# Attention joined into two visits per chunk, with quarter-array state products, in a fused decay-attention and two-stage MoE kernel

## The chip, the core and the metric

The kernel runs on one core of one Trainium2 chip. The core has five engines: TensorE (PE in the profile, with PEld for its weight loads), VectorE (DVE), ScalarE (ACT), GpSimd (POOL) and SyncE (SP), whose queue issues most DMAs. The metric is the device time of one execution in microseconds (us), as the median of several runs.

## The reference

Attention with a decaying state feeds a dense squared-ReLU MLP, and that feeds a noisy top-2 mixture of eight experts:

```python
f = sigmoid(f_logit)                               # 4 batches, 8 heads, 768 steps, D = 48
for t in range(S):
    state = f[:, :, t, :, None] * state + einsum('bhd,bhe->bhde', k[:, :, t], v[:, :, t])
    y[:, :, t] = einsum('bhd,bhde->bhe', q[:, :, t], state)
x = y.transpose(0, 2, 1, 3).reshape(3072, 384)
h = maximum(x @ w_in, 0); x = (h * h) @ w_out      # 384 -> 2048 -> 384
noisy = x @ w_gate + log1p(exp(x @ w_noise)) * noise
# for each token its two largest experts, weighted by softmax: relu(x @ w1[e]) @ w2[e]
```

## The kernel before

**Tiling.** Tokens come in 24 chunks of 128 (`NCH`), six for each batch (`NCB`), and in eight blocks of three chunks (384 tokens, `NBLK`). Two heads share the 128 partitions as a pair, at partitions 0 to 47 and 64 to 111, and there are four pairs (`HP`).

**Attention of a chunk** is five pieces, `att_units(c)`: `a_A` (products of keys and queries, masked on VectorE into AM), `a_k` (transposes of the keys, copied by ScalarE into KT), `a_U` (the chunk's contribution to the state, then added and scaled on VectorE), `a_Y(c, 0)`, and `a_Y(c, 1)` followed by `a_S`. `a_Y` adds AM times values for half of the pairs each time; its second call also adds the products of the state `S_t` with the queries, which are full 128x128 matmuls, since `S_t` holds a pair's two states on its diagonal and zeros elsewhere. `a_S` refreshes `S_t`. The last chunk of a batch has no `a_k`, `a_U` and `a_S`, the first has no state product.

**The dense MLP** runs in units u: `mm1(u)` (nine matmuls into the bank mm, then r, g, gh on ScalarE and gl on VectorE) and `mm2(u - 2)` (nine matmuls into the banks a0 to a2). Each of the blocks 2 to 7 has 16 units. Up to u = 31 a list written out by hand, `ORDER`, sets the order of loads (W, E, V), weight conversion (A, H, B), preparation of chunks (P), attention pieces (a) and units (M). From u = 32 a loop does so: each unit calls `mm1`, then `attend`, which gives out one attention piece per unit, then `mm2`, then whatever `at` has put down for that unit. So a piece stands on TensorE between nine matmuls of `mm1` and nine of `mm2`: this is called a visit below. Chunk 10 is the first whose pieces all fall in the loop.

**Other steps** put down by `at`: `r_store` (VectorE turns a finished block into x2q, which is stored), `r_logits`, `r_logits2`, `r_exp`, `r_ln`, `r_choose`, `r_share`, `r_slots`, `r_scatter` (routing of the block's tokens, ending in six indirect DMAs from GpSimd), `check_load` and `check_step` (a test of the weights' words, one load and one VectorE step for each of 16 pieces), `zeros_out` and `pads` (fills in DRAM). `pads` writes small entries from a tile of the tag x2b, which `r_store`, `r_rows` and others share with one buffer.

**PSUM** has eight banks: mm twice, a0 to a2, and t0 to t2, which `abank` hands out in turn to attention and routing.

**Preparation** of a chunk: `prep_f`, then `prep_k` and `prep_F` (a scan on VectorE, and a small ScalarE copy FE of its result), `prep_G`, `prep_q` with `prep_Q` (on GpSimd).

Engines run their instructions in order, and so does SP's queue of DMAs.

Of the kernel before, what the change touches and what calls it, by code (L numbers as in the profile page):

```python
# [227 lines left out]
def kernel(  # L228
# [159 lines left out]
    def w_load(i):  # L388
# [8 lines left out]
        if kind == "in":  # L397
            for (r0, m, row0, rs) in ((0, 48, 0, 96), (64, 48, 48, 96), (48, 16, 288, 16), (112, 16, 336, 16)):
                s = bass.AP(tensor=w_in_v.tensor, offset=w_in_v.offset + row0 * DFF * WORDS + p * n,
                            ap=[[DFF * WORDS, m], [rs * DFF * WORDS, 3], [1, n]])  # L400
                nc.sync.dma_start(st[r0:r0 + m], s)
# [57 lines left out]
    phase = {"early": True}  # L459

    def abank(shape, dt=F32):
# [58 lines left out]
    def prep_F(c):  # L520
# [25 lines left out]
    def a_k(c):  # L546
        if c % NCB == NCB - 1:
            return
        pk = abank([128, HP, 128])
# [5 lines left out]
    def a_A(c):  # L555

        pA = [abank([128, HP, 128]) for s in range(2)]
# [10 lines left out]
    def a_U(c):  # L568
        if c % NCB == NCB - 1:
            return  # L570
        pU = abank([128, HP, D])
# [13 lines left out]
    def a_S(c):  # L585
        if c % NCB == NCB - 1:
            return
        for s in range(2):
            r = slice(64 * s, 64 * s + D)
            nc.scalar.activation(S_t[r, :, r], S_c[r], AF.Copy)  # L590

    pY = {}

    def a_Y(c, h):
        if h == 0:
            pY[c] = abank([128, HP, 128])
# [12 lines left out]
        if h == 1:  # L609
# [6 lines left out]
            if c >= 2 * BT:  # L616
                t = LP["p"].tile([128, HP, C], F32, tag="xs", name="xs", bufs=2)
                nc.scalar.activation(t, py, AF.Copy)
# [111 lines left out]
    def r_logits(j):  # L730

        pl = abank([128, BTOK])
# [5 lines left out]
    def r_logits2(j):  # L738
        pl = abank([128, BT, 96])
# [108 lines left out]
    def r_slots(j):  # L848
        oh, wt, ohb, cb, s12 = R[j]
        den = share_out(wt, s12, BT)  # L850
        pr = abank([128, BT, E])
# [345 lines left out]
    def pads():  # L1197
        t = mp.tile([128, NTL, E, 4], F32, tag="x2b", name="pads", bufs=1)
# [62 lines left out]

    if wide:
# [168 lines left out]
```

## Time and profile before

| what | value |
|---|---|
| median of 3 runs | 1038.68 us (1034.66 to 1039.46) |
| the profiled execution | 1035.95 us, span 1034.2 us |
| TensorE busy | 974.7 us (94% of the span), 6378 matmul instructions |
| VectorE, ScalarE, GpSimd busy | 617.0, 491.7, 183.0 us |
| mean granted TensorE clock | 0.976 of full speed |
| chain that ended last | PE 78%, DVE 6%, DMA 5%, SP's queue 4%, ACT 3% |

The span is the profiled part; 1.75 us lie around it. The chain follows the last instruction back through whatever released each step, so a share of 78% for PE says that most of the time the end was set by TensorE working through its own queue.

### The profile page before, as it was taken

To read this page: it belongs to the slowest core of one execution; us is meant where nothing else is said; L and a number is where in the kernel's file an instruction comes from. 1 tells how busy PE (TensorE), PEld (TensorE's weight loads), DVE (VectorE), ACT (ScalarE), POOL (GpSimd) and SP (SyncE) were. 2 spreads that over 40 slices of the span, in tenths; PEclk is the share of its full clock that TensorE was granted. 3 is DMA by queue.
4 is the path that set the end of the run, shared out by engine and by line. 5 is a ranking of instruction groups with operands and counts; after the bars stand their busy time and mean duration, and the time that the engine had idled before them with its cause. 6 is when DMAs were issued, how large, how long until landed. Compare 5 with 4: busy or idle time off the path is not lost.

```text
span 1034.2 us, 17267 instructions
## 1 busy us (share of the span) xinstructions
PE 974.7 (94%) x6378; PEld 903.2 (87%) x6378; DVE 617.0 (60%) x1297; ACT 491.7 (48%) x1026; POOL 183.0 (18%) x282
## 2 busy tenths in 40 slices
PE   4679999799899999999999999999999999999994
PEld 3568899689789999999999989999989899999984
DVE  6999897678678777677326573354535343535320
ACT  2455544365555555565657743354434343434320
POOL 2000000002301303114030204211212121212112
PEclk9879999899999999999999999999999999999997
DMA  9897837657665866644044646664837465656212
GB/s 176 162 173 174 184 96 111 130 145 212 193 177 133 250 171 182 149 113 119 23 120 103 174 115 106 125 125 81 152 67 138 81 121 98 110 95 116 26 19 33
DMA packets 186110, 131.30 MB, mean 127 GB/s; under 512 B 113440, under 2 KB 170400, under 8 KB 186016
## 3 DMA queue, kind: packets, MB, share of 16 engines
q1 hardware_dynamic: 173696, 107.59, 47.2%
q0 software_dynamic: 10368, 19.37, 10.5%
q10 hardware_dynamic: 1952, 3.15, 1.1%
q8 instruction: 52, 0.85, 0.4%
q14 instruction: 42, 0.34, 0.1%
HBM read 93.45 MB, written 34.25 MB: 123 GB/s over the span
## 4 chain that ended last, share of the span: by engine, by line
PE 78%; DVE 6%; DMA 5%; SPq 4%; ACT 3%; issue 2%; POOL 0%; DVEq 0%; POOLq 0%; ACTq 0%
PE mm L1000 20%; PE a L698 15%; PE mm L665 14%; PE a L1062 8%; PE a L1045 7%; PE t L1062 3%; DMA st_in<-in_moe_w_in_dram 2%; PE t L604 2%; PE t L608 2%; PE t L560 1%; PE a L1032 1%; SPq L483 1%; SPq L356 1%; PE t L576 1%; PE t L1079 1%
## 5 line engine op out<-in xcount | busy, mean ns | idle before, releaser
L665 PE MATMUL mm<-x,inh 128*128 128x384 f32 x768 | 200.3, 342 | 1.1 <-ACT r L668 1.0
L1012 DVE SCALAR_TENSOR_TENSOR hl<-mm,hh 128x288 fp32r<-128x288 f32 (+1 forms) x120 | 67.9, 566 | 164.7 <-ACT hh L1011 157.2
L665 PEld LDWEIGHTS mm<-x,inh 128*128 128x128 f32 x768 | 137.9, 189 | 6.7 <-issue 4.9
L1088 POOL DMA_INDIRECT out_dram<-y,tt x56 | 88.8, 1585 | 307.8 <-ACT y L1086 300.0
L698 PE MATMUL a<-gl,outh 128*128 128x384 f32 x384 | 130.3, 339 | 9.9 <-DVE gl L678 9.9
L698 PE MATMUL a<-gh,outh 128*128 128x384 f32 x384 | 136.1, 354 | 2.8 <-ACT x2T L709 2.8
L1000 PE MATMUL mm<-gxh,eh 128*128 128x288 f32 (+1 forms) x384 | 134.4, 350 | 0.0
L678 DVE TENSOR_TENSOR gl<-g,gh 128x384 fp32r<-128x384 f32 x128 | 72.5, 568 | 102.4 <-ACT gh L673 73.3
L1000 PE MATMUL mm<-gxh,el 128*128 128x288 f32 (+1 forms) x384 | 132.8, 346 | 0.0
L1000 PE MATMUL mm<-gxl,eh 128*128 128x288 f32 (+1 forms) x384 | 132.7, 346 | 0.0
L1011 ACT ACTIVATE hh<-mm 128x288 fp32r<-128x288 f32 (+1 forms) x120 | 59.6, 497 | 149.6 <-PE mm L1000 138.8
L665 PE MATMUL mm<-x,inl 128*128 128x384 f32 x384 | 130.1, 339 | 0.0
L698 PE MATMUL a<-gh,outl 128*128 128x384 f32 x384 | 130.0, 339 | 0.0
L668 ACT ACTIVATE r<-mm 128x384 f32<-128x384 f32 x128 | 62.0, 485 | 90.4 <-PE mm L665 67.8
L544 POOL TENSOR_TENSOR qT<-qT,F 128x512 f32<-128x512 f32 x18 | 24.3, 1350 | 346.5 <-DVE qT L468 297.6
L698 PEld LDWEIGHTS a<-gl,outh 128*128 128x128 f32 x384 | 72.9, 190 | 10.9 <-DVE gl L678 10.8
L698 PEld LDWEIGHTS a<-gh,outh 128*128 128x128 f32 x384 | 72.7, 189 | 8.2 <-ACT x2T L709 3.1
L1000 PEld LDWEIGHTS mm<-gxh,el 128*128 128x128 f32 x384 | 72.1, 188 | 8.7
L1000 PEld LDWEIGHTS mm<-gxh,eh 128*128 128x128 f32 x384 | 72.2, 188 | 6.1 <-DVE hl L1012 0.2
L1000 PEld LDWEIGHTS mm<-gxl,eh 128*128 128x128 f32 x384 | 72.3, 188 | 5.9
L698 PEld LDWEIGHTS a<-gh,outl 128*128 128x128 f32 x384 | 72.8, 190 | 0.0
L665 PEld LDWEIGHTS mm<-x,inl 128*128 128x128 f32 x384 | 72.6, 189 | 0.0
(239 smaller groups left out, 1971.5 us busy)
## 6 DMA issues: line engine op xcount, KB each, us to landing
est<-in_moe_w_dram SPq DMA_DIRECT2D x56, 192.0 KB
est<-in_moe_w_dram SPq DMA_DIRECT2D x14, 768.0 KB
gr<-slotted SPq DMA_DIRECT2D x96, 96.0 KB
ck<-in_moe_w_in_dram SPq DMA_DIRECT2D x8, 768.0 KB
ck<-in_moe_w_out_dram SPq DMA_DIRECT2D x8, 768.0 KB
out_dram<-zeros SPq DMA_DIRECT2D x46, 128.0 KB
v<-in_v_dram SPq DMA_DIRECT2D x24, 192.0 KB
st_out<-in_moe_w_out_dram SPq DMA_DIRECT2D x6, 768.0 KB
```

The lines of the kernel that those rows point to most:

```text
L544: eng.tensor_tensor(qT[c], PT.pop((c, "q")) if c < EARLY else qT[c], F, op=OP.mult)
L604: nc.tensor.matmul(py[64 * s:64 * s + 64, p, :], vv[:, (2 * p + s) * D:(2 * p + s) * D + 64], AM[c][s][:, p, :], start=(p == 0), stop=(fir ...
L665: nc.tensor.matmul(ph, a[:, c, fs], b_[:, c, :], start=(n == 0), stop=(n == 8))
L668: nc.scalar.activation(r, ph, AF.Relu)
L678: nc.vector.tensor_sub(gl, g, gh.bitcast(F32))
L698: nc.tensor.matmul(acc[j][d], a[:, f % 4, ds_], b_, start=(first and n == 0), stop=(last and n == 2))
L1000: nc.tensor.matmul(ph[:, :n], a[:, c, fs], b_[:, c, o:o + n], start=(i == 0), stop=(i == 8))
L1011: nc.scalar.activation(hh[:, :n], ph[:, :n], AF.Relu)
L1012: nc.vector.scalar_tensor_tensor(hl[:, :n], ph[:, :n], 0.0, hh[:, :n].bitcast(F32), op0=OP.max, op1=OP.subtract)
L1045: nc.tensor.matmul(ya[d], a[:, f % 4, d * 128:d * 128 + 128], b_[:, :n], start=(f == 0 and i == 0), stop=(last and i == 2))
L1062: nc.tensor.matmul(ya[t][:m], a[:, ts_], b_[:, f % 4, :], start=(f == 0 and i == 0), stop=(last and i == 2))
L1088: st = nc.gpsimd.indirect_dma_start(out=out, out_offset=bass.IndirectOffsetOnAxis(ap=slots(e, T)[:m, 0:1].bitcast(I32), axis=0), in_=y[:m] ...
```

## The change

From chunk 10 (`MERGED`) a chunk's five pieces become two visits: `a_A` with `a_k`, and two units later `a_U`, `a_Y(c, 0)`, `a_Y(c, 1)`, `a_S` together. From chunk 12 (`QUARTERS`) the second visit has the order `a_Y`, `a_Y`, `a_U`, `a_S`, and the state products are eight matmuls of 48 rows by 64 columns, each on a quarter of the array, in two banks. For that the two heads of an odd pair swap their halves of the output in all chunks (`out_half`), so the rows of `w_in` are loaded in another order, by six DMAs in place of four, and `a_S` makes four small copies in place of two before chunk 12, and one from there on. In the loop the banks are fixed by tag up to u = 111 (A and Y in t0 and t1, transposes, U and routing in t2).

FE is copied one unit later (in `prep_G`) from chunk 6 on. `pads` uses the tile ck in place of x2b. `check_load` and `check_step` come every five units in place of four. `r_store` comes two units later for blocks 3 to 7. For blocks 2 to 5 `r_logits` and `r_logits2` stand right ahead of the attention visit of their unit (4 and 9 units after u0, in place of 1 and 4), `r_slots` 14 units after u0 in place of 11, `r_scatter` likewise.

```diff
@@ w_load
-            for (r0, m, row0, rs) in ((0, 48, 0, 96), (64, 48, 48, 96), (48, 16, 288, 16), (112, 16, 336, 16)):
+            for (r0, m, row0, rs, cs) in ((0, 48, 0, 192, slice(0, 3, 2)), (0, 48, 144, 0, slice(1, 2)),
+                                          (64, 48, 48, 192, slice(0, 3, 2)), (64, 48, 96, 0, slice(1, 2)),
+                                          (48, 16, 336, 16, slice(0, 3)), (112, 16, 288, 16, slice(0, 3))):
...
@@ abank
-    def abank(shape, dt=F32):
+    def abank(shape, dt=F32, tag=None):
+        if tag and phase["merged"]:
+            return bank(tag, shape, dt)
...
@@ prep_F, prep_G
-        nc.scalar.activation(FE[:, c, :], F[:, :, C - 1], AF.Copy)
+        if c < EARLY:
+            nc.scalar.activation(FE[:, c, :], F[:, :, C - 1], AF.Copy)
...
+        if c >= EARLY:
+            nc.scalar.activation(FE[:, c, :], Fp[c][:, :, C - 1], AF.Copy)
@@ a_U, a_S
-        pU = abank([128, HP, D])
+        pU = abank([128, HP, D], tag="t2" if c >= QUARTERS else "t1")
...
+        if c >= QUARTERS:
+            nc.scalar.activation(S_t[:, :, 0:D], S_c, AF.Copy)
+            return
         for s in range(2):
             r = slice(64 * s, 64 * s + D)
-            nc.scalar.activation(S_t[r, :, r], S_c[r], AF.Copy)
+            for odd in range(2):
+                o = 64 * (s ^ odd)
+                nc.scalar.activation(S_t[r, odd::2, o:o + D], S_c[r, odd::2], AF.Copy)
+    QUARTERS = 2 * EARLY
+    def out_half(p, s):
+        return 64 * (s ^ (p & 1))
@@ a_Y
+        two = c >= QUARTERS
         if h == 0:
-            pY[c] = abank([128, HP, 128])
-        py = pY[c]
+            pY[c] = ([bank("t0", [128, 2, 128]), bank("t1", [128, 2, 128])] if two else
+                     abank([128, HP, 128], tag="t0"))
+        py = [pY[c][p % 2][:, p // 2, :] if two else pY[c][:, p, :] for p in range(HP)]
...
-                nc.tensor.matmul(py[64 * s:64 * s + 64, p, :], vv[:, (2 * p + s) * D:(2 * p + s) * D + 64],
-                                 AM[c][s][:, p, :], start=(p == 0), stop=(first and p == HP - 1))
+                o = out_half(p, s)
+                nc.tensor.matmul(py[p][o:o + 64], vv[:, (2 * p + s) * D:(2 * p + s) * D + 64], AM[c][s][:, p, :],
+                                 start=(p == 0 or (two and p == 1)), stop=(first and p >= HP - 1 - two))
         if h == 1 and not first:
             for p in range(HP):
-                nc.tensor.matmul(py[:, p, :], S_t[:, p, :], qT[c][:, p, :], start=False, stop=(p == HP - 1))
+                if not two:
+                    nc.tensor.matmul(py[p], S_t[:, p, :], qT[c][:, p, :], start=False, stop=(p == HP - 1))
+                    continue
+                for s in range(2):
+                    r, o = slice(64 * s, 64 * s + D), out_half(p, s)
+                    nc.tensor.matmul(py[p][o:o + 64], S_t[r, p, 0:64], qT[c][r, p, :], start=False,
+                                     stop=(p >= HP - 2))
...
@@ pads
-        t = mp.tile([128, NTL, E, 4], F32, tag="x2b", name="pads", bufs=1)
+        t = LP["p"].tile([128, NTL, E, 4], F32, tag="ck", name="pads", bufs=1)
@@ units
+    MERGED = 10
     for c in range(NCH):
-        units += [(c, i, [w]) for i, w in enumerate(att_units(c))]
+        ws = [[w] for w in att_units(c)]
+        if c >= MERGED:
+            late = ws[2] + ws[3] + ws[4]
+            if c >= QUARTERS:
+                late = [lambda c=c: (a_Y(c, 0), a_Y(c, 1), a_U(c), a_S(c))]
+            ws = [[], [], ws[0] + ws[1], [], late]
+        units += [(c, i, w) for i, w in enumerate(ws)]
...
@@ check and routing
-            at(2 * NF + 4 * i, check_load, i)
-            at(2 * NF + 4 * i + 3, check_step, i)
+            at(2 * NF + 1 + 5 * i, check_load, i)
+            at(2 * NF + 1 + 5 * i + 3, check_step, i)
...
-        at(u0, r_store, j)
+        at(u0 + 2 * (j > 2), r_store, j)
...
+        if 1 < j < NBLK - 2:
+            beside(u0 + 4, r_logits, j)
+            beside(u0 + 9, r_logits2, j)
+            at(u0 + 9, r_rows, j)
+            for w, d in zip(steps[1:], (9, 9, 10, 10, 10, 13, 14, 14)[1:]):
+                (beside if w is r_slots else at)(u0 + d, w, j)
+            continue
```

How this moves instructions is seen in each engine's order. On TensorE, before, in the units that hold block 2's `r_logits` (t<-x2T,wgn) and chunk 13's `a_U` (t<-v,KT):

```order
L698 MATMUL a_4069<-gh,outl_309 128x384
L734 MATMUL t_4080<-x2T,wgn 32x384 [waits DVE_49]
L734 MATMUL t_4080<-x2T,wgn 32x384 x2
L665 MATMUL mm<-x,inh_557 128x384 x2
L665 MATMUL mm<-x,inl_558 128x384
L665 MATMUL mm<-x,inh_557 128x384 x2
L665 MATMUL mm<-x,inl_558 128x384
L665 MATMUL mm<-x,inh_557 128x384 x2
L665 MATMUL mm<-x,inl_558 128x384
L576 MATMUL t_4104<-v_118,KT 64x48 [waits DVE_49,Activation_49]
L576 MATMUL t_4104<-v_118,KT 64x48 x7
L698 MATMUL a_4067<-gh,outh_308 128x384
```

The products of AM and of the state follow one and two units later. In the changed kernel the same pieces of chunk 13 stand in one visit (L629 is AM times values, L638 the state products, L585 `a_U`):

```order
L700 MATMUL mm<-x,inl_572 128x384
L769 MATMUL t_4208<-x2T,wgn 32x384 [waits Activation_49]
L769 MATMUL t_4208<-x2T,wgn 32x384 x2
L629 MATMUL t_4214<-AM,v_118 64x128 [waits DVE_49] x2
L629 MATMUL t_4215<-AM,v_118 64x128 x2
L629 MATMUL t_4214<-AM,v_118 64x128 x2
L629 MATMUL t_4215<-AM,v_118 64x128 x2
L638 MATMUL t_4214<-qT,S_t 64x128 x2
L638 MATMUL t_4215<-qT,S_t 64x128 x2
L638 MATMUL t_4214<-qT,S_t 64x128 x2
L638 MATMUL t_4215<-qT,S_t 64x128 x2
L585 MATMUL t_4235<-v_118,KT 64x48 [waits Activation_49]
```

So the three separate visits and the routing visit have become one, with eight quarter matmuls in place of four full ones. On VectorE, before, at u = 25, where `r_store` of block 1 makes x2q:

```order
L675 TENSOR_TENSOR g<-r 128x384 [waits Activation_49]
L678 TENSOR_TENSOR gl<-g,gh 128x384 [waits DVE_49,Activation_49]
L719 STREAM_TRANSPOSE x2q<-x2T 128x3x12x32 [waits DMAHW4_49,DMAHW3_49,DMAHW5_49,DMAHW2_49,DMAHW6_49,DMAHW1_49,DMAHW7_49,Activation_49,Pool_49]
L675 TENSOR_TENSOR g<-r 128x384 [waits Activation_49]
L678 TENSOR_TENSOR gl<-g,gh 128x384 [waits DVE_49,PE_49,Activation_49]
```

The same place in the changed kernel:

```order
L710 TENSOR_TENSOR g<-r 128x384 [waits Activation_49]
L713 TENSOR_TENSOR gl<-g,gh 128x384 [waits DVE_49,Activation_49]
L754 STREAM_TRANSPOSE x2q<-x2T 128x3x12x32 [waits Activation_49]
L710 TENSOR_TENSOR g<-r 128x384 [waits Activation_49]
L713 TENSOR_TENSOR gl<-g,gh 128x384 [waits DVE_49,PE_49,Activation_49]
```

Nothing moved there, but the waits for seven DMAs, those of `pads`, are gone. On ScalarE, before, the copy FE stands ahead of the unit's r, g and gh (u = 49, with x2T of block 2 behind them):

```order
L618 ACTIVATE xs<-t_3857 128x512 [waits PE_49]
L590 ACTIVATE S_t<-S 48x4x48 x2
L526 ACTIVATE FE<-F 128x4 [waits DVE_49]
L668 ACTIVATE r<-mm 128x384 [waits PE_49]
L672 ACTIVATE g<-r 128x384 [waits Activation_49]
L673 ACTIVATE gh<-g 128x384 [waits Activation_49]
```

In the changed kernel it stands behind them:

```order
L651 ACTIVATE xs<-t_3952 128x2x128 [waits PE_49]
L598 ACTIVATE S_t<-S 128x4x48 [waits DVE_49]
L703 ACTIVATE r<-mm 128x384 [waits PE_49]
L707 ACTIVATE g<-r 128x384 [waits Activation_49]
L708 ACTIVATE gh<-g 128x384 [waits Activation_49]
L540 ACTIVATE FE<-F 128x4 [waits DVE_49]
```

FE has moved behind one unit's work on the same engine.

## Rows read from the trace of the kernel before

**Rows 1.** Busy time by stretch: us, each engine (instructions), PEclk, DMA share, GB/s.

```profile
0.00:50.00 50.00, 28.18 (x246) 23.60 (x247) 37.82 (x62) 17.99 (x36) 5.27 (x41) 0.90 1.03 170
...
290.00:560.00 270.00, 269.40 (x1876) 249.33 (x1876) 175.87 (x438) 156.82 (x336) 49.11 (x71) 1.00 0.52 139
590.00:1034.00 444.00, 430.50 (x2583) 402.18 (x2581) 187.49 (x379) 173.65 (x354) 97.03 (x123) 0.99 0.51 94
```

**Rows 2.** Timeline of TensorE, separate visits: start, us, line, out<-in, count.

```profile
310.62 0.34 PE L665 MATMUL mm<-x,inl 128*128 128x384 f32 x1
310.89 0.67 PE L576 MATMUL t<-v,KT 128*64 128x48 f32 x16
...
311.77 0.34 PE L698 MATMUL a<-gl,outh 128*128 128x384 f32 x1
...
314.55 0.34 PE L665 MATMUL mm<-x,inl 128*128 128x384 f32 x1
314.82 0.66 PE L604 MATMUL t<-AM,v 128*64 128x128 f32 x8
...
315.69 0.34 PE L698 MATMUL a<-gl,outh 128*128 128x384 f32 x1
...
318.47 0.34 PE L665 MATMUL mm<-x,inl 128*128 128x384 f32 x1
...
319.32 1.16 PE L608 MATMUL t<-qT,S_t 128*128 128x128 f32 x8
...
320.50 0.34 PE L698 MATMUL a<-gl,outh 128*128 128x384 f32 x1
```

**Rows 3.** The same view, an early visit in which the pieces already stand together.

```profile
156.93 0.34 PE L698 MATMUL a<-gh,outl 128*128 128x384 f32 x1
157.20 0.67 PE L576 MATMUL t<-v,KT 128*64 128x48 f32 x16
157.70 1.06 PE L604 MATMUL t<-AM,v 128*64 128x128 f32 x16
158.69 1.16 PE L608 MATMUL t<-qT,S_t 128*128 128x128 f32 x8
...
160.04 0.34 PE L665 MATMUL mm<-x,inl 128*128 128x384 f32 x1
160.21 0.51 PE L665 MATMUL mm<-x,inh 128*128 128x384 f32 x2
```

**Rows 4.** The same view; in brackets the idle time before and what ended it.

```profile
189.73 0.69 PE L698 MATMUL a<-gl,outh 128*128 128x384 f32 x1 [7.14 <-DVE gl L678]
190.21 0.52 PE L698 MATMUL a<-gh,outl 128*128 128x384 f32 x1
190.53 0.52 PE L698 MATMUL a<-gh,outh 128*128 128x384 f32 x1
...
284.14 0.45 PE L698 MATMUL a<-gh,outh 128*128 128x384 f32 x1 [2.82 <-ACT x2T L709]
```

**Rows 5.** Timeline of VectorE.

```profile
187.16 1.38 DVE L719 STREAM_TRANSPOSE x2q<-x2T 128x1152 f32<-128x1152 f32 x1 [11.66 <-DMA raw_f<-in_f_logit_dram]
...
197.57 1.10 DVE L468 STREAM_TRANSPOSE fT<-raw_f 128x512 f32<-128x512 f32 x1
...
355.34 1.37 DVE L719 STREAM_TRANSPOSE x2q<-x2T 128x1152 f32<-128x1152 f32 x1
```

**Rows 6.** Timeline of SP's queue: start, us that the issues took, count.

```profile
63.25 1.76 SPq L401 DMA_DIRECT2D st_in<-in_moe_w_in_dram  x4
...
172.93 6.08 SPq L1202 DMA_DIRECT2D slotted<-pads  x7
```

**Rows 7.** Timeline of ScalarE.

```profile
274.75 0.72 ACT L590 ACTIVATE S_t<-S 48x192 f32<-48x192 f32 x2
281.40 0.21 ACT L526 ACTIVATE FE<-F 128x4 f32<-128x4 f32 x1 [5.93 <-issue]
```

**Rows 8.** Timeline of GpSimd, the last of block 2's six scatters.

```profile
344.58 0.96 POOL L886 DMA_INDIRECT slotted<-rows,sli  x1 [0.22 <-issue]
```

More of the change, by code (lines that the diff above doesn't have):

```diff
@@ L397, in w_load @@
         if kind == "in":
-            for (r0, m, row0, rs) in ((0, 48, 0, 96), (64, 48, 48, 96), (48, 16, 288, 16), (112, 16, 336, 16)):
+            for (r0, m, row0, rs, cs) in ((0, 48, 0, 192, slice(0, 3, 2)), (0, 48, 144, 0, slice(1, 2)),
+                                          (64, 48, 48, 192, slice(0, 3, 2)), (64, 48, 96, 0, slice(1, 2)),
+                                          (48, 16, 336, 16, slice(0, 3)), (112, 16, 288, 16, slice(0, 3))):
+                d = st[r0:r0 + m, cs, :]
                 s = bass.AP(tensor=w_in_v.tensor, offset=w_in_v.offset + row0 * DFF * WORDS + p * n,
-                            ap=[[DFF * WORDS, m], [rs * DFF * WORDS, 3], [1, n]])
-                nc.sync.dma_start(st[r0:r0 + m], s)
+                            ap=[[DFF * WORDS, m], [rs * DFF * WORDS, d.shape[1]], [1, n]])
+                nc.sync.dma_start(d, s)
         else:
@@ L458 @@
     P2 = {}
-    phase = {"early": True}
-    def abank(shape, dt=F32):
+    phase = {"early": True, "merged": False}
+    def abank(shape, dt=F32, tag=None):
+        if tag and phase["merged"]:
+            return bank(tag, shape, dt)
         rot[0] += 1
@@ L548, in a_k @@
             return
-        pk = abank([128, HP, 128])
+        pk = abank([128, HP, 128], tag="t2")
         for p in range(HP):
@@ L555, in a_A @@
     def a_A(c):
-        pA = [abank([128, HP, 128]) for s in range(2)]
+        pA = [abank([128, HP, 128], tag=f"t{s}") for s in range(2)]
         for p in range(HP):
@@ L617, in a_Y @@
                 t = LP["p"].tile([128, HP, C], F32, tag="xs", name="xs", bufs=2)
-                nc.scalar.activation(t, py, AF.Copy)
+                if two:
+                    for odd in range(2):
+                        nc.scalar.activation(t[:, odd::2, :], pY[c][odd], AF.Copy)
+                else:
+                    nc.scalar.activation(t, pY[c], AF.Copy)
                 pY[c] = t
@@ L730, in r_logits @@
     def r_logits(j):
-        pl = abank([128, BTOK])
+        pl = abank([128, BTOK], tag="t2")
         for c in range(3):
@@ L738, in r_logits2 @@
     def r_logits2(j):
-        pl = abank([128, BT, 96])
+        pl = abank([128, BT, 96], tag="t2")
         t = LG.pop(j)
@@ L850, in r_slots @@
         den = share_out(wt, s12, BT)
-        pr = abank([128, BT, E])
+        pr = abank([128, BT, E], tag="t2")
         nc.tensor.matmul(pr, before, ohb, start=True, stop=False)
@@ L1260, in at, with beside @@
         extra.setdefault(u, []).append((fn, a))
+    def beside(u, fn, a):
+        mid.setdefault(u, []).append((fn, a))
     if wide:
         for i in range(NCK):
-            at(2 * NF + 4 * i, check_load, i)
-            at(2 * NF + 4 * i + 3, check_step, i)
+            at(2 * NF + 1 + 5 * i, check_load, i)
+            at(2 * NF + 1 + 5 * i + 3, check_step, i)
     for step in range(3):
@@ L1281 @@
         at(u0 - 4, n_load, j)
-        at(u0, r_store, j)
+        at(u0 + 2 * (j > 2), r_store, j)
         if j == NBLK - 1:
-            mid[u0 + 1] = j
-        else:
+            mid[u0 + 1] = [(r_logits, j)]
+        steps = (r_logits2, r_exp, r_exp2, r_ln, r_choose, r_share, r_slots, r_scatter)
+        if 1 < j < NBLK - 2:
[5 more added lines that the diff above has]
+            continue
+        if j < NBLK - 1:
             at(u0 + 1 + (j == 0), r_logits, j)
-        steps = (r_logits2, r_exp, r_exp2, r_ln, r_choose, r_share, r_slots, r_scatter)
         for w, d in zip(steps, SPREAD[max(0, j - NBLK + 3)]):
@@ L1364 @@
     for u in range(2 * NF, NU + NEU + LAG):
+        phase["merged"] = u < (NBLK - 1) * NF
         if u == (NBLK - 1) * NF:
@@ L1373 @@
             emm1(u - NU)
-        if u in mid:
-            r_logits(mid.pop(u))
+        for fn, a in mid.pop(u, []):
+            fn(a)
         j, f = divmod(u, NF)
```

## Prediction

> **What bounds the kernel now.** I read the busy time by stretch first. From 290 us to 560 us, where most of the changed chunks lie, TensorE is busy 269.40 of 270 us, VectorE 175.87 and ScalarE 156.82; in the experts' stretch behind it TensorE is busy 430.50 of 444 us [rows 1]. So in both the end moves by whatever TensorE is spared, as long as no other engine comes late. The first 50 us are another matter: TensorE is busy 28.18 us, VectorE 37.82, and the DMA engines' share is 1.03 [rows 1], so there it is data that is waited for. Then I read TensorE's timeline, where two kinds of loss stand: the gaps around each attention visit, which are small and many [rows 2], and two long idle times, 7.14 and 2.82 us [rows 4].
>
> **What a visit costs.** Inside the MLP one matmul starts .17 us after the other [rows 3]. The cost of a visit is the time from the start of the last matmul ahead of it to that of the second one behind it, less two such steps (.35). For `a_U` that is 311.77 - 310.62 - .35 = .80; for half of the AM products 315.69 - 314.55 - .35 = .79; for the other half with the state products 320.50 - 318.47 - .35 = 1.68 [rows 2]. Together 3.27. In the early visit where all of these stand together it is 160.04 - 156.93 less three steps (.52) = 2.59 [rows 3]. Joining thus saves .68. The joined visit less the visit of 1.68 is .91, the work of `a_U` and of one half; alone they cost 1.59. So each visit pays .34 for going in and coming out, .17 for each change between the MLP's 128*128 shape and the attention's 128*64. What is left is .46 for `a_U`, .45 for half of AM, and 1.68 - .45 - .34 = .89 for the state products, whose shape is the MLP's.
>
> **Quarters.** No row shows four quarters at work. The nearest rows are the AM products, which use halves of the array: 16 instructions from 157.70 to 158.69, .062 each, where the full-array state products take .11 each (8 from 158.69 to the next start, .91 in all) [rows 3]; two halves thus run side by side. If four quarters do likewise, the 16 instructions of the state products take half of .89, .45; if only two run at a time, the whole .89. I take .45, as the halves come close to their ideal. But the order AM, state in quarters, `a_U` changes shape twice more. The new second visit is four changes (.68), AM .90, state .45, `a_U` .46: 2.49.
>
> The Trainium skill, TensorEngine Tiling (Array Packing), section Tiling Modes, says that a change of tiling mode drains the engine; the .17 per change above agrees. It is what speaks against the quarters here: by the rule ten visits gain about .1 each and not .45, and were the two inner changes free, the sum below would be 3.1 us lower.
>
> **Sum of the visits.** Eight chunks (13 to 16, 19 to 22) go from 3.27 to 2.49: 6.2. Chunk 10, joined without quarters: .7. Chunks 12 and 18, without state products, from .80 + .79 + .79 to .46 + .90 + .34: .7 each. Chunk 11, the last of its batch and not in quarters, loses one entry and exit: .3. Chunks 17 and 23 go from .79 + 1.68 to .34 + .17 + .90 + .45: .6 each. Together 9.8. Bounds: 5.4 where the state products keep .89 in ten chunks, 12.9 where the inner changes are free. Joining `a_A` and the transposes changes shape between them still, so I take nothing, with .34 for 11 chunks (3.7) as the other bound. The four `r_logits` that now stand against a visit save one change each, .7; the `r_logits2` nothing to .34 each, taken as nothing.
>
> **The idle time of 7.14 us.** It ends with gl, and VectorE was late because x2q stood 11.66 us on a wait [rows 4, 5]. The row names a load of raw_f, but x2q reads no such tile; it takes over the buffer x2b from `pads`, whose seven DMAs were issued from 172.93 on for 6.08 us [rows 6], and the order shows seven DMA waits on it. The changed kernel has none. Behind the gap eight matmuls start .32 apart in place of .17 [rows 4], a further 1.2. So 8.3 us go. What is late next is the transpose of raw_f at 197.57 [rows 5]; without the gap it would stand at about 189, just behind the landing at 187.16. I take 8.0, with 4 as a lower bound, should that load come later still.
>
> **The idle time of 2.82 us** ends with x2T [rows 4], and ScalarE was late by FE, on which it stood 5.93 us [rows 7] for VectorE's scan. FE now stands a unit later, and the load that held VectorE (ck) is issued nearer to its place. I take 3.5 with the slow matmuls behind it; bounds 0 and 4.
>
> **What it costs.** Six loads in place of four for each of eight pieces of `w_in`: four issues take 1.76 us [rows 6], so 16 more take 7.0 us of SP's queue. Where SP waits for data in any case (share 1.03 [rows 1]) they cost nothing; I take 1.5, bounds 0 and 7.0. Two more copies of S_t in each early chunk: two take .72 us [rows 7], hidden while ScalarE is busy 17.99 of 50 us [rows 1]; if the cover is gone, .7 for each of some nine, 6; I take nothing. In two chunks (14, 20) `a_U` now waits for t2 until VectorE has reduced `r_logits2`'s products, queued behind gl; nothing is the lower bound, a visit's 2.49 the upper; I take .5 each, 1.0. TensorE's `mm2` is queued behind it and bears it in full. The check's steps, the copies of two halves in place of one, and the routing steps lie on engines with a third of their time free [rows 1] and are priced at nothing.
>
> **Sum:** -9.8 - .7 - 8.0 - 3.5 + 1.5 + 1.0 = -19.5, from the profiled execution's 1035.95 to 1016.4. The median of the runs shown lies 2.7 above that execution; between the two I predict 1018 us.
>
> **Rivals.**
> *The quarters do not run four at a time.* For it: no row shows them. Against: halves do run side by side [rows 3]. The visits then save 5.4: 1022 us.
> *The start pays for the loads.* The issues cost 7.0, not 1.5, since SP's queue issues one after the other and what is behind them comes later; if the 2.82 us stay as well, 1027 us. Against: the DMA engines are full there [rows 1].
> *Joined visits find their operands late.* AM, KT and the bank t2 now have two units in place of three, and each wait stands in TensorE's own queue. If each of 14 second visits waits .7, the joining is undone: 1028 us. Against: two units are over 6 us, and VectorE and ScalarE have a third of their time free [rows 1].
> *Slower: x2q waits for the scatter.* Both use x2b. Before, block 2's last scatter began at 344.58 and the next x2q at 355.34, 9.8 us after its end [rows 5, 8]. Now `r_scatter` comes three units later and `r_store` two, so a unit of some 3.1 us less, and 6.7 are left for the scatter to land. From more than that on, VectorE stands as at 187.16. If four blocks (3 to 6) each lose the 8.3 us of the first gap, 33 us come back: 1051 us, slower than before. It needs VectorE to stand about ten us in each.
>
> **How the numbers follow.** Chances: the forecast (1011 to 1024) .60; two at a time .15; the start .12; late operands .09; the scatter .04. A tenth on either side is left out by 1009 to 1029, which takes in 12.9 and part of 3.7 of gain on the low side and the start and late operands on the high side. About .5% (5 us) is what a measurement of this kernel can tell from no change. All cases but the last lie below 1033; their upper tails reach within it: faster .92, same .04, slower .04.
>
> **What would show it.** Two visits per chunk, the second near 2.5 us (2.9 if two at a time) and the state products' 16 instructions within .5 us; no wait on the first x2q and no gap near 180 us; no wait of ScalarE on FE; the unit with `r_logits2` waiting under 1 us at `a_U`. Wrong it would be if units before u = 20 start later by more than 2 us (the loads), or if x2q of blocks 3 to 6 stands on GpSimd's DMAs.

## The result, and the profile after

The changed kernel takes 1027.97 us (median of 4 runs, 1027.60 to 1029.13) beside 1037.56 us for the kernel before on the same chip: a ratio of 0.991, with a 95% interval of 0.989 to 0.994. That is a gain of 9.6 us where I had forecast 19.5. The profiled execution takes 1028.07 us, its span is 1026.3 us.

First the busy time by stretch, in stretches that answer to those of [rows 1] (columns as there).

```profile
0.00:50.00 50.00, 27.60 (x232) 22.91 (x234) 37.16 (x61) 18.60 (x42) 5.27 (x41) 0.78 1.04 170
280.00:550.00 270.00, 260.92 (x1948) 245.13 (x1948) 180.13 (x442) 152.22 (x335) 53.82 (x71) 0.99 0.52 139
582.00:1026.00 444.00, 430.76 (x2585) 402.59 (x2584) 186.85 (x378) 173.31 (x353) 97.01 (x123) 0.99 0.50 94
```

In the middle stretch TensorE was busy 269.40 of 270 us before; now it is idle for 9 of them. So much of what the visits were to spare comes back as idle time, and the next question is where. The view of TensorE's waits (waiting tile and line, what it waited for; us in total, times, longest) names the places. Of the groups behind the start those are shown that are new or have grown, and ahead of them the one of gl, which was 9.9 us before (7.14 of it the gap of [rows 4], which is gone) and now lies at other units.

```profile
PE a L733 <- DVE gl L713: 7.0, 4, 4.2
...
PE mm L700 <- ACT r L703: 4.0, 3, 1.8
PE t L585 <- DVE rb L896: 3.7, 2, 2.6
PE t L585 <- DVE lt L779: 2.5, 2, 1.3
...
PE t L585 <- ACT lgT L771: 1.1, 3, 0.5
```

Line 585 is `a_U`; rb, lt and lgT are what the three routing steps (`r_slots`, `r_logits2`, `r_logits`) make from their products. All three products lie in the bank t2, which `a_U` now needs too: 7.3 us in seven visits.

To follow the time through the kernel I take the start of each unit, that is of the first of its nine products at L700 (L665 before), and subtract one trace from the other. The start of unit 28 differs by some us from one execution to the next (179.09 to 182.22 us in the twelve traces with the changed loads), so the differences are set to nought there (180.69 us before, 180.38 after). Negative is earlier than in the kernel before:

```
unit             29     50     51     52     54     80    111    125    127   experts   end
changed       -9.08 -13.07 -18.41 -18.25 -11.10 -13.10 -11.31 -10.64  -7.39   -7.27   -7.56
```

Five things stand in it: 9.1 gained at unit 29 and 5.3 at 51, the places of the two idle times of the forecast; 4.0 gained between them, where the first joined visits lie; 7.1 lost at units 53 and 54; almost nothing gained from 54 to 111, where ten chunks with the new visits lie; 3.3 lost at units 126 and 127, where I expected nothing.

**A visit.** The timeline of TensorE, a second visit that waits for nothing.

```profile
463.17 0.34 PE L700 MATMUL mm<-x,inl 128*128 128x384 f32 x1
463.44 1.09 PE L629 MATMUL t<-AM,v 128*64 128x128 f32 x16
464.46 0.67 PE L638 MATMUL t<-qT,S_t 48*64 48x128 f32 x16
465.15 0.67 PE L585 MATMUL t<-v,KT 128*64 128x48 f32 x16
465.75 0.45 PE L733 MATMUL a<-gh,outh 128*128 128x384 f32 x1
466.04 0.33 PE L733 MATMUL a<-gl,outh 128*128 128x384 f32 x1
```

By the measure of the prediction it costs 466.04 - 463.17 - .35 = 2.52 (forecast 2.49). The quarters take .69 from their first start to that of `a_U`. But of the ten such visits with an `a_U` seven wait for t2, and the longest wait is in the next one, of the same view: `a_U` stands 2.56 us until VectorE has read the slots' products out of t2.

```profile
394.28 0.34 PE L700 MATMUL mm<-x,inl 128*128 128x384 f32 x1
394.55 1.09 PE L629 MATMUL t<-AM,v 128*64 128x128 f32 x16
398.20 0.67 PE L585 MATMUL t<-v,KT 128*64 128x48 f32 x16 [2.56 <-DVE rb L896]
```

**Units 53 and 54.** From the timelines of SP's queue, GpSimd, VectorE and TensorE, one line or two of each:

```profile
255.18 0.58 SPq L1140 DMA_DIRECT2D ck<-in_moe_w_in_dram  x1
256.49 0.38 SPq L912 DMA_DIRECT2D rows<-x2s  x1
...
264.11 1.88 POOL L921 DMA_INDIRECT slotted<-rows,sli  x1 [10.99 <-DMA rows<-x2s]
...
268.19 0.46 SPq L1140 DMA_DIRECT2D ck<-in_moe_w_in_dram  x1
...
271.57 0.96 POOL L921 DMA_INDIRECT slotted<-rows,sli  x1 [0.23 <-issue]
...
277.93 1.38 DVE L754 STREAM_TRANSPOSE x2q<-x2T 128x1152 f32<-128x1152 f32 x1 [8.76 <-DMA slotted<-rows,sli]
...
279.80 0.44 PE L733 MATMUL a<-gl,outh 128*128 128x384 f32 x1 [4.21 <-DVE gl L713]
```

Block 2's x2q takes the buffer in which block 0's rows still lie, stands 8.76 us until their scatter has landed, and gl behind it stops TensorE. Two loads of ck go out about there: one ahead of rows, the next among the six scatters. The first two scatters landed 4.1 and 4.4 us after their start, the last two, which started behind that second load, 6.7 and 6.0 us. The first x2q has no wait any more, where [rows 5] had one of 11.66:

```profile
174.83 1.37 DVE L754 STREAM_TRANSPOSE x2q<-x2T 128x1152 f32<-128x1152 f32 x1
```

**Units 126 and 127.** SP's queue, ScalarE and TensorE:

```profile
543.83 12.66 SPq L972 DMA_DIRECT2D gr<-slotted  x4
...
560.67 0.53 ACT L988 ACTIVATE gxh<-gT 128x384 fp32r<-128x384 f32 x1 [3.96 <-DVE gT L985]
...
568.05 0.63 ACT L372 ACTIVATE eh<-est 128x512 fp32r<-128x512 f32 x1 [1.05 <-DMA est<-in_moe_w_dram]
...
570.88 0.62 PE L700 MATMUL mm<-x,inh 128*128 128x384 f32 x2 [1.82 <-ACT r L703]
```

The first tokens for the experts (gr) come late, the flips behind them (gT) come late, and ScalarE, where r is queued behind them, comes late for TensorE. In the kernel before the same four fetches of gr took 1.94 us.

### The profile page after: what moved, and what is told of

Its sections match the earlier page's. It is cut to its first block, busy times and chain, and to the rows that moved or that the text cites. A ratio compares the mean times of both kernels' runs of the same rounds, so it can differ in the third digit from the quotient of the medians.

```text
span 1026.3 us, 17480 instructions
## 1 busy us (share of the span) xinstructions
PE 962.4 (94%) x6458; PEld 899.5 (88%) x6458; DVE 617.5 (60%) x1297; ACT 491.1 (48%) x1048; POOL 189.2 (18%) x282
## 4 chain that ended last, share of the span: by engine, by line
PE 69%; DVE 10%; DMA 7%; ACT 5%; SPq 4%; issue 3%; POOL 1%; DVEq 0%; POOLq 0%; ACTq 0%
PE mm L1035 20%; PE a L733 12%; PE mm L700 12%; PE a L1097 8%; PE a L1080 7%; PE t L1097 3%; DMA st_in<-in_moe_w_in_dram 2%; PE a L1067 1%; PE t L569 1%; ACT g L707 1%; DVE fT L474 1%; ACT r L703 1%; PE t L629 1%; SPq L356 1%; DMA raw_q<-in_q_dram 1%
## 5 line engine op out<-in xcount | busy, mean ns | idle before, releaser
L700 PE MATMUL mm<-x,inh 128*128 128x384 f32 x768 | 199.0, 340 | 4.0 <-ACT r L703 4.0
L700 PEld LDWEIGHTS mm<-x,inh 128*128 128x128 f32 x768 | 138.3, 189 | 7.0 <-ACT r L703 5.1
L733 PE MATMUL a<-gh,outh 128*128 128x384 f32 x384 | 132.3, 344 | 0.0
L713 DVE TENSOR_TENSOR gl<-g,gh 128x384 fp32r<-128x384 f32 x128 | 75.0, 588 | 94.7 <-ACT gh L708 91.3
L700 PE MATMUL mm<-x,inl 128*128 128x384 f32 x384 | 129.7, 338 | 0.0
L921 POOL DMA_INDIRECT slotted<-rows,sli x48 | 53.2, 1109 | 140.3 <-DVE rows L905 70.2
L700 PEld LDWEIGHTS mm<-x,inl 128*128 128x128 f32 x384 | 72.4, 189 | 0.0
```

Source lines behind the costliest of these rows:

```text
L700: nc.tensor.matmul(ph, a[:, c, fs], b_[:, c, :], start=(n == 0), stop=(n == 8))
L713: nc.vector.tensor_sub(gl, g, gh.bitcast(F32))
L733: nc.tensor.matmul(acc[j][d], a[:, f % 4, ds_], b_, start=(first and n == 0), stop=(last and n == 2))
L921: st = nc.gpsimd.indirect_dma_start(out=slotted, out_offset=bass.IndirectOffsetOnAxis(ap=sli[:, i, s:s + 1], axis=0), in_=x[:, i, :], in_o ...
```

## Experiments

The unit differences below are against the kernel before, set to nought at unit 28, unless another kernel is named. Ratios are to the kernel before as run on the same chip. The changed kernel was not run beside the experiments, and the intervals of the ratios reach 2 to 4 us to either side; so a difference of a few us between it and one experiment is not shown by the whole times, and is read from one trace of each. Where two programs are the same, most steps from unit to unit agree to a few hundredths of a us; the exceptions that bear on a reading are named.

**1. pads back in x2b.**

```diff
-        t = LP["p"].tile([128, NTL, E, 4], F32, tag="ck", name="pads", bufs=1)
+        t = mp.tile([128, NTL, E, 4], F32, tag="x2b", name="pads", bufs=1)
```

> As the changed kernel, but pads again lies in the buffer x2b. Theory G (the stall at unit 28 is a loss by itself): x2q stands about 11 us again, unit 29 starts 8.5 to 9 us later than in the changed kernel, and all of it stays to the end: about 1036.5. Theory H (what is spared early is given back at the next x2q, whose wait ends when block 0's scatter has landed, whatever came before): the same 9 us at unit 29, but the stall of 7.1 us at units 53 and 54 shrinks by as much, and the time is about 1030. The scatter of block 0 hangs on units 43 to 45, which move too, so the place where G and H part is the step at units 53 and 54.

Measured 1036.81 us, ratio 1.003 (1.001 to 1.005). The first x2q waits again, and TensorE behind it (VectorE, then TensorE):

```profile
185.24 1.38 DVE L754 STREAM_TRANSPOSE x2q<-x2T 128x1152 f32<-128x1152 f32 x1 [9.38 <-DMA raw_f<-in_f_logit_dram]
...
187.80 0.69 PE L733 MATMUL a<-gl,outh 128*128 128x384 f32 x1 [4.58 <-DVE gl L713]
```

Unit 29 starts 6.7 us later than in the changed kernel, counted from unit 28, and unit 54 6.8: the stall at 53 and 54 did not shrink. Theory G. The other 2.4 of the 9.1 us at unit 29 do not come back, and in experiment 2, where pads lies in x2b too, they are gone as well; so they are not shown to be the buffer's. The traced execution lost another 3.2 us at units 115 and 116 (below).

**2. The kernel before with FE a unit later, and nothing else.** The edit is the diff's for `prep_F` and `prep_G`.

> The kernel before, with one edit of the change alone: FE is written a unit later from chunk 6 on. Theory I (one lateness behind another): the wait of 2.8 us on x2T goes, worth 4 to 5 us at unit 51, but block 2's x2q, which in the kernel before started at 287.36 when block 0's scatter had just landed, now stands on that scatter, and TensorE loses 4 to 6 us at units 52 to 54; the time is that of the kernel before within 1 us. Theory J (the two are apart): the gain of 4 to 5 us at unit 51 stays to the end.

Measured 1029.93 us, ratio 0.995 (0.994 to 0.997). From unit 50 to unit 52 it gains 4.5 us on the kernel before, and keeps them to the experts; 2.4 at unit 29 and .8 at unit 46 come ahead of that, but this execution reached unit 28 4.0 us later. x2q stands .71 us there, and the trace doesn't put even that down to the scatter:

```profile
285.83 1.38 DVE L722 STREAM_TRANSPOSE x2q<-x2T 128x1152 f32<-128x1152 f32 x1 [0.71 <-ACT lgT L739]
```

Theory J, not I. FE is worth 4.5 us by itself, and something else in the change makes x2q meet the scatter.

**3. Block 2's x2q four units later.**

```diff
-        at(u0 + 2 * (j > 2), r_store, j)
+        at(u0 + (2 * (j > 2) or 4 * (j == 2)), r_store, j)
```

> Block 2's x2q is written four units later than in the changed kernel, nothing else. Theory C (x2q stands 8.8 us on block 0's scatter, and gl behind it stops TensorE at units 52 to 54 for about 7 us): the wait on x2q and the steps at units 53 and 54 go, and the time falls by 5 to 7 us, to about 1022. Theory D (TensorE is stopped there by r and by gl for the work of the units itself; x2q is only next in the queue): less than 2 us. A third possibility is that the gain is taken back by the next block: x2q of block 3 would then stand on block 2's scatter, by some us.

Measured 1024.62 us, ratio 0.992 (0.990 to 0.994). x2q no longer waits, and unit 54 starts 6.2 us earlier than in the changed kernel: theory C.

```profile
285.48 1.38 DVE L754 STREAM_TRANSPOSE x2q<-x2T 128x1152 f32<-128x1152 f32 x1
```

The stall is no accident of one execution: the seven traces in which x2q keeps its place and the check its new pace (the changed kernel, experiments 1, 5, 6 and 7, the two runs of 8) lose 6.2 to 7.4 us at units 53 and 54. 1.5 us are lost again at units 81 and 82, but the two runs of experiment 8, whose program is the changed kernel's up to there, lose them too; so they are not x2q's.

**4. The check at its old pace.**

```diff
-            at(2 * NF + 1 + 5 * i, check_load, i)
-            at(2 * NF + 1 + 5 * i + 3, check_step, i)
+            at(2 * NF + 4 * i, check_load, i)
+            at(2 * NF + 4 * i + 3, check_step, i)
```

> The changed kernel, with the check's loads and steps (ck) at the pace of the kernel before, every fourth unit, so that no ck load stands between x<-y and block 0's rows on SP's queue; nothing else. Theory K (block 2's x2q finds block 0's scatter unfinished because rows is issued later against its unit): rows is issued about 1.3 to 2.5 us earlier, the wait of 8.8 us on x2q and the 7.1 us at units 53 and 54 shrink by about as much, and the time is 1.5 to 2.5 us less. Theory L (x2q only comes too early, since the visits and FE ahead of it were made shorter): the wait stays within 1 us of 8.8 and nothing is gained.

Measured 1026.13 us, ratio 0.991 (0.989 to 0.994). Now rows goes out ahead of ck, and the first scatter starts 3.5 us sooner, counted from unit 28. The next load of ck goes out when the last scatter has been started, and x2q has no wait (SP's queue, GpSimd, VectorE):

```profile
256.22 0.38 SPq L912 DMA_DIRECT2D rows<-x2s  x1
258.60 0.43 SPq L1140 DMA_DIRECT2D ck<-in_moe_w_in_dram  x1
...
261.25 1.15 POOL L921 DMA_INDIRECT slotted<-rows,sli  x1 [6.41 <-DMA rows<-x2s]
...
268.04 1.96 POOL L921 DMA_INDIRECT slotted<-rows,sli  x1 [0.22 <-issue]
...
270.12 0.43 SPq L1140 DMA_DIRECT2D ck<-in_moe_w_in_dram  x1
...
272.58 1.37 DVE L754 STREAM_TRANSPOSE x2q<-x2T 128x1152 f32<-128x1152 f32 x1
```

Not L, and K by its direction, but by more than K forecast. Counted from unit 28, the scatter has landed at least 6.0 us sooner, of which 3.5 come with the earlier data. The rest, which K did not have, may lie in the second load of ck, which now goes out behind the scatters; no run parts the two. x2q itself also comes 2.8 us later here, which hides what may be left of the wait. Unit 54 starts 3.5 us earlier than in the changed kernel, not 7: the check's step at its old place holds VectorE 3.73 us for ck's data at 265.27, where the changed kernel's 3.68 us lay at 260.78, and 2.7 us of the stall that moving FE had removed are back at unit 51. So the check's new pace both helped at unit 51 and cost at 53.

**5. No quarters.** The value of `QUARTERS` alone: `a_U` stands first, on t1; Y has t0; the states' products use the whole array.

```diff
-    QUARTERS = 2 * EARLY
+    QUARTERS = NCH
```

> As the changed kernel, but all joined second visits keep the states' products on the whole array (QUARTERS past the last chunk), so a_U stands first in the visit and on the bank t1, and Y on t0 alone. By the rows: a second visit without waits costs 2.59 (as chunk 10) against 2.52 with quarters, so the quarters themselves are worth .07 in each of eight visits, .6 us in all; and a_U no longer waits for t2, which is worth 7.3. Theory A (the waits for t2 are a loss of their own): time falls by about 6.5 us, to about 1021.5. Theory B (they only show a lateness that is there in any case): time rises by .6, to about 1028.5, with the waits at another line. If quarters were worth .45 in a visit, 3.6 us less of gain in either case.

Measured 1026.30 us, ratio 0.992 (0.988 to 0.995). No wait on rb, lt or lgT at L585 is left. The visit that answers to the one shown above:

```profile
459.18 0.34 PE L700 MATMUL mm<-x,inl 128*128 128x384 f32 x1
459.45 0.67 PE L585 MATMUL t<-v,KT 128*64 128x48 f32 x16
459.95 1.06 PE L629 MATMUL t<-AM,v 128*64 128x128 f32 x16
460.94 1.16 PE L634 MATMUL t<-qT,S_t 128*128 128x128 f32 x8
461.86 0.42 PE L733 MATMUL a<-gh,outh 128*128 128x384 f32 x1
462.12 0.34 PE L733 MATMUL a<-gl,outh 128*128 128x384 f32 x1
```

462.12 - 459.18 - .35 = 2.59. Against the changed kernel the visits in which that one waits for t2 gain 1.18, 1.02, .23, 2.77, .20 and 1.15 (the steps to units 59, 65, 70, 81, 86 and 91), 6.55 in all; visits without such a wait lose .07 to .15, those of chunks 17 and 23, without `a_U`, .29. At unit 83 1.4 of the gain go again; the other kernel without quarters and with joined visits (experiment 9) loses them there too, so they belong to the count. From unit 54 to 111 4.2 us are left. Theory A: the quarters give some 1.4 us in ten visits (8 times .1 and twice .29), and the waits that they bring cost four times that, 4.2 + 1.4 = 5.6. The edit changes the bank of `a_U` and its place in the visit together; which of the two frees it is not shown. The whole time fell by less, and units 115 and 116 cost 1.6 more in this execution.

**6. The routing out of t2's way, quarters kept.** For blocks 2 to 5:

```diff
-            beside(u0 + 4, r_logits, j)
-            beside(u0 + 9, r_logits2, j)
+            at(u0 + 4, r_logits, j)
+            at(u0 + 9, r_logits2, j)
             at(u0 + 9, r_rows, j)
-            for w, d in zip(steps[1:], (9, 9, 10, 10, 10, 13, 14, 14)[1:]):
+            for w, d in zip(steps[1:], (9, 10, 11, 11, 11, 12, 13, 13)[1:]):
```

> For blocks 2 to 5 the routing products leave the way of the second visits: r_logits and r_logits2 stand behind the unit's mm2 instead of ahead of the visit, and r_slots a unit earlier, so that the bank t2 is free when a_U asks for it. Theory A (the visits' gain was eaten by a_U's waits for t2, 7.3 us in the changed kernel): the waits of TensorE at a_U fall from 7.3 us to under 1.5, the separate entries of eight small products cost .34 each (up to 2.7) more, and the time falls by 4.5 to 6 us, to about 1023. Theory B (VectorE and ScalarE are late there in any case, and t2 is only where it shows): the waits move to another line (gl, r or KT) and the time stays within 2 us of 1028.

Measured 1030.83 us, ratio 0.998 (0.996 to 0.999): no gain, and by the units the end comes 2.3 us later than in the changed kernel. The waits at `a_U` are gone, but `r_slots` itself now stands in TensorE's queue for the choice of experts; I had moved the one a unit earlier and the other a unit later (the view of waits):

```profile
PE t L887 <- DVE ohb L873: 7.1, 5, 2.3
```

This looks like theory B, but the waiting line is one that my own edit made late; it does not decide between A and B.

**7. `a_U` in the free half of t1, behind the odd pairs' Y.**

```diff
-        pU = abank([128, HP, D], tag="t2" if c >= QUARTERS else "t1")
+        if c >= QUARTERS:
+            pU = pY[c, "u"]
+        else:
+            pU = abank([128, HP, D], tag="t1")
...
-            pY[c] = ([bank("t0", [128, 2, 128]), bank("t1", [128, 2, 128])] if two else
-                     abank([128, HP, 128], tag="t0"))
+            if two:
+                b1 = bank("t1", [128, 512])
+                pY[c] = [bank("t0", [128, 2, 128]), b1[:, 0:256].rearrange("p (a t) -> p a t", a=2)]
+                pY[c, "u"] = b1[:, 256:256 + HP * D].rearrange("p (a d) -> p a d", a=HP)
+            else:
+                pY[c] = abank([128, HP, 128], tag="t0")
```

> As the changed kernel, but in chunks with quarters a_U writes into the free half of the bank t1, behind the odd pairs' Y, instead of into t2; nothing is moved. Theory A: the 7.3 us of waits at a_U on t2 fall under 1, no visit gets longer otherwise, and the time falls by 6 to 7 us, to about 1021.5. Theory B (VectorE or ScalarE late in any case): the waits move to the next line that needs them (KT, gl or r), and the time stays within 2 us of 1028. A third: a_U, whose bank is also read by ScalarE for Y, makes that copy wait and the next first visit (which takes t0 and t1) late, by some .3 us a visit.

Measured 1038.31 us, ratio 1.003 (1.001 to 1.006). The third case of the expectation, and by more than it says: `a_U` now waits in ten visits until ScalarE has copied Y out of the same tile.

```profile
PE t L588 <- ACT xs L658: 11.3, 10, 2.8
```

That is more than t2 cost. It shows what sharing that tile with Y costs here, and nothing on A and B.

**8. The stall at units 126 and 127.** SP's queue stands 12.66 us in the first fetch of gr. The program's list of instructions with their waits says what its fourth transfer waits for (three of tt and the four gr on SP, then the first est on ScalarE):

```
L951 DMA tt_6501<-slotted 128x2x4 [waits DMAHW6_49]
L951 DMA tt_6501<-slotted 128x2x4 [waits DMAHW7_49]
L951 DMA tt_6501<-slotted 128x2x4 [waits DMAHW1_49]
L972 DMA gr<-slotted 32x8x96 [waits DMAHW2_49]
L972 DMA gr<-slotted 32x8x96 [waits DMAHW4_49]
L972 DMA gr<-slotted 32x8x96 [waits DMAHW6_49]
L972 DMA gr<-slotted 32x8x96 [waits DMAHW0_49]
...
L1000 DMA est<-in_moe_w_dram 32x3x512 [waits DVE_49]
```

In the list each transfer waits on a completion counter (DMAHW0, DMAHW1 and so on) that an earlier transfer has used. My reading is that DMAHW0, on which the fourth gr waits, was last given to the first load of est. That load waits for VectorE, which has to free its buffer, and is issued at 553.23 only. The list does not show who has the counter; the second of the next two runs tests it. The two: block 6's x2q back at its old unit, and that load of est a unit later.

```diff
-        at(u0 + 2 * (j > 2), r_store, j)
+        at(u0 + 2 * (2 < j < 6 or j == 7), r_store, j)
```

> Block 6's x2q is written at its old unit, two earlier than in the changed kernel, nothing else. Theory E (the stall of 3.3 us at units 126 and 127 comes from rows and gr being issued two units later behind x2s): the steps at those units go and the time falls by about 3 us, to about 1025. Theory F (the first gr fetch stands 12.7 us on SP because its fourth transfer waits for the same completion counter as a load of est on ScalarE's queue, and that does not change here): the fourth gr still stands until about 556 us, and the time stays within 1 us of 1028.

Measured 1030.80 us, ratio 0.997 (0.995 to 0.999); gr stands 16.87 us, and the steps at units 126 and 127 stay (2.1 and 1.3). Not theory E.

```diff
-        dict(l=(-16, -16, -8, -6), s=(-12, -10, -6, -5), g=(-11, -10, 9, 9), f=(-7, -6, -5, -4, 12, 13, 14)),
+        dict(l=(-16, -16, -7, -6), s=(-12, -10, -6, -5), g=(-11, -10, 9, 9), f=(-7, -6, -5, -4, 12, 13, 14)),
```

> The first load of est on ScalarE's queue stands one unit later in the program, behind the first gr fetch, so that the fourth gr no longer shares a completion counter with it; nothing else. Theory F: the four gr are issued in about 2 us instead of 12.7, the first flip (gT) starts some 2 us earlier against its unit, the steps of +2.0 and +1.3 us at units 126 and 127 go or shrink below 1 us, and the time falls by 2 to 3 us, to about 1025.5. Theory E: no change, within 1 us of 1028.

Measured 1027.88 us, ratio 0.995 (0.993 to 0.997). Theory F was right on SP's queue and wrong on the time: the four transfers go out in 1.94 us and the first flip is 1.0 us earlier, counted from unit 28, but now ScalarE waits longer for est (1.48 and 1.77 us against one wait of 1.05), and the steps stay at 1.9 and 1.3. SP's queue, then ScalarE:

```profile
544.08 1.94 SPq L972 DMA_DIRECT2D gr<-slotted  x4
...
562.07 0.63 ACT L372 ACTIVATE eh<-est 128x512 fp32r<-128x512 f32 x1 [1.48 <-DMA est<-in_moe_w_dram]
...
568.25 0.63 ACT L372 ACTIVATE eh<-est 128x512 fp32r<-128x512 f32 x1 [1.77 <-DMA est<-in_moe_w_dram]
```

**9. Three edits together, with and without joining, and two with quarters.** The edits are 3 and 5, and the load of tt a unit earlier, which by the same reading parts gr from est's counter without moving est:

```diff
-    at(uE + 2, t_load, "tt0", 4, 2)
+    at(uE + 1, t_load, "tt0", 4, 2)
```

> The changed kernel with three edits: no quarters (a_U first, on t1), block 2's x2q four units later, and the load of tt a unit earlier, which puts it and x2s ahead of est's first load, so that the fourth gr no longer shares a counter with a load of est while est's load stays where it was. If the three losses are separate ones: -4.2 (as between units 54 and 108 without quarters) -6.0 (as at units 53 and 54 with x2q late) -3.3 (units 126 and 127), about -13 from the changed kernel's 1028, so 1015, and the fetch of gr takes 2 us. If the stall at units 126 and 127 has to do with est's loads and not with the counter: 1018.

The second run also takes the joining away:

```diff
-    MERGED = 10
+    MERGED = NCH
...
-        phase["merged"] = u < (NBLK - 1) * NF
+        phase["merged"] = False
```

> The same three edits, and no chunk joined (MERGED past the last chunk, banks taken in turn as in the kernel before): five visits' pieces stand apart, all else as in the run with the three edits. By the prediction's rows joining alone is worth .7 in each of eleven chunks with a_U, and .3 to .6 in the others, some 8 us (9.8 less 1.4 for the quarters): it should be 8 us slower than the joined kernel, about 1023, spread evenly over units 33 to 108 at 1.3 to 1.4 per entry spared. If joined visits mostly make operands late, the difference is under 4 us, and the joined kernel shows waits at L569, L585 or L700 that this one lacks.

> The changed kernel, quarters and all, with two edits: block 2's x2q four units later and the load of tt a unit earlier. If the losses are separate: -6.0 and -3.3, about 1019; against the run with three edits the 7.3 us of waits at a_U on t2 stay, less .1 to .3 a visit that the quarters are worth, so it should be some 4 us slower than that one.

Measured: with the three edits 1020.47 us, ratio 0.988 (0.986 to 0.991), the fastest of all; the same not joined 1030.01 us, ratio 0.997 (0.995 to 0.998); with quarters and two edits 1025.92 us, ratio 0.994 (0.992 to 0.996). These three ran on the same chip, so their times compare as they are: not joining costs 9.5 us, the quarters 5.5. By units:

```
unit                    50     51     54     80    111    117    125    127   experts   end
three edits         -13.06 -18.40 -17.56 -21.57 -21.97 -18.57 -18.57 -16.05  -15.93  -15.87
same, not joined     -9.91 -14.81 -14.94 -13.45 -12.91  -9.67  -9.19  -6.92   -6.81   -5.81
two, quarters       -13.07 -18.41 -16.40 -18.41 -15.07 -11.65 -11.65  -8.96   -8.83   -9.31
```

At unit 111 the joined kernel is 21.97 - 12.91 = 9.1 us ahead of the same kernel not joined: joining pays what the rows said, and not under 4. By chunk it is .6 to .8 in eight of the eleven with an `a_U`, .3 to .4 in the last chunk of each batch, and uneven in chunks 15, 18 and 19 (1.5, 1.3 and -.7). The one without quarters is 21.97 - 15.07 = 6.9 ahead of the one with them; of this 1.2 come at unit 54, and 1.5 at unit 81 beyond the wait of the changed kernel there; without these two it is the 4.2 of experiment 5. Against the changed kernel the three edits gain 21.97 - 11.31 = 10.7 up to unit 111, and experiments 3 and 5 had 6.2 and 4.2 there: up to unit 111 the losses are separate. Behind it, all three lose 3.0 to 3.2 us at units 115 and 116, and the stall at 126 and 127 is still 2.3 to 2.7: gr goes out in 2.6 us, but the next load of est is late instead (ScalarE in the run with three edits).

```profile
558.10 0.63 ACT L372 ACTIVATE eh<-est 128x512 fp32r<-128x512 f32 x1 [2.97 <-DMA est<-in_moe_w_dram]
```

## Why the prediction failed, step by step

- **Visits, -9.8: right.** Joining is worth 9.1 (unit 111, experiment 9), quarters 1.4 (experiment 5): together 10.5, the waits for t2 apart. The visit of 2.49 measured 2.52. The -.7 for `r_logits` is in no run by itself: in experiment 9 both kernels have it beside the visit, and in experiment 6 other waits cover it.
- **Quarters: right, four at a time.** .69 from their first start to the next piece's is .52 and one change of shape, beside .45 taken; so the rival with two at a time falls. A visit gained .07 to .15, not .45; .45 less two changes of .17 would be .11. The Trainium skill, TensorEngine Tiling (Array Packing), section Tiling Modes, has it that a change of the mode drains the engine; the small gain agrees with it.
- **The stall of 7.14 us, -8.0: right.** -9.1 at unit 29; back by 6.7 with pads in x2b. Both other traces with pads in x2b lack the remaining 2.4 (experiments 1 and 2); what they hang on stays open.
- **The stall of 2.82 us, -3.5: a little small.** -5.3 at unit 51; 4.5 from FE alone, and with the check's old pace 2.7 of them are lost, so the check has its part.
- **The loads, +1.5: too dear.** The changed kernel reaches unit 28 .31 us earlier than the one before, and the twelve traces with the new loads at 179.09 to 182.22, where the kernel before has 180.69. The rival in which the start pays falls; between 0 and 1.5 the traces do not decide.
- **`a_U` behind `r_logits2`, +1.0: the first step that failed.** I priced the bank t2 in two chunks, for one routing step. All three steps hold it, `r_slots` a unit ahead of a visit, and seven visits waited 7.3 us. The quarters' second bank for Y takes t1 from `a_U`; so this is the quarters' price. Net of what comes back at unit 83 it is 5.6 us, four times what they give (experiments 5 and 9).
- **"The check's steps ... and the routing steps ... are priced at nothing": the second.** I looked at the share of busy time and not at the queue. One load of ck came to stand ahead of block 0's rows on SP, and the next among their scatters; the scatter landed late, x2q waited 8.8 us, and 7.1 us were lost, of which experiment 3 gives back 6.2. My slower rival had this mechanism, with the same buffer, but I looked for it in blocks 3 to 6, whose steps the change moves, and gave it .04. It came at block 2, whose x2q isn't moved: what was ahead of it got shorter, and what it waits for got later. Experiments 3 and 4 both remove the wait; experiment 2 shows that FE alone doesn't bring it, and experiment 1 that it is there with the first stall as well as without. How much of it each load of ck makes is not shown.
- **Units 126 and 127, +3.3: not in the sum at all.** Open in part. That gr waited on est's counter is borne out by the run with est later, but without that wait est's own loads come late, and 2.3 to 3.2 us stay. That the loads of gr, rows and est hold one another up there is my reading; no run tried it.

The sum by measured terms, from unit 28 to the experts: -9.1 - 5.3 - 10.5 + 7.1 + 7.3 + 3.3 = -7.2, where -7.27 was measured. That the two agree to a tenth is luck. The terms overlap: .45 of the 5.3 is a joined visit's, .9 of the 7.1 stays when x2q no longer waits, and 1.4 of the 7.3 comes back at unit 83; and .7 lost between units 111 and 125 is in none of them. What stands is their size: the terms of gain were within 2 us of their forecast, and what failed were the waits, of which I had counted 1.0 and there were some 15 to 18.

## What to carry to other kernels

When a change gives a shared bank or buffer one more user, list every holder of it over a whole period and ask of each when it lets go, not only of the one that stands next. A step priced at nothing because its engine is half idle still has a place in a queue: read what is issued behind it there, and who waits for that. And when stalls ahead of a step go, check the waits of the steps that are not moved: they arrive earlier at data that do not.

## What the runs showed of the hardware

- Quarters of the array run side by side, and by their time four of them: 16 instructions of 48*64 take .69 us to the next piece's start, a change of shape included, where 16 of 128*64 in the same visit take 1.02 (464.46 - 463.44) and 8 of 128*128 take .92 (461.86 - 460.94).
- A transfer on one queue can be held by one on another. The four fetches of gr took 1.94 us of SP's queue in place of 12.66 when a load on ScalarE's queue stood a unit later in the program, and nothing else was changed.
- In six traces units 115 and 116 cost more than in the changed kernel: 3.0 to 3.2 us in experiments 1 and 7 and the three runs of 9, 1.6 in experiment 5. In all six ScalarE stood 2.34 to 2.41 us ahead of lgT there, where the changed kernel's stood .75, and the trace names only "remote" as the cause. The edits of experiments 1, 5 and 7 touch nothing at these units (those of 9 move one load there); it stays open.
